# A stored order of all steps replaced by another, in a fused attention and two-layer feed-forward kernel

## The chip, the cores and the metric

The kernel runs on one core of a Trainium2 chip. The metric is the time of one execution on the device in microseconds (us). The profile is one such execution, recorded by the hardware profiler.

## What is computed

Three stages follow each other. Four batches of eight heads attend over 576 positions in a window (the first four heads: the last 32 positions; the other four: every fourth of the last 128). The result, 2304 tokens of 512 numbers, goes through a first feed-forward block with a softmax gate and a layer norm, and then through a second block with a GELU.

```
scores = scale * np.matmul(q, k.transpose(0, 1, 3, 2))          # 4 x 8 x 576 x 576
scores = np.where(masks[None, :, :, :], scores, -1000000000.0)
attn = softmax(scores);  x = np.matmul(attn, v)                 # 2304 x 512

h = x @ w_in                                                    # 512 -> 1024
solu = h * softmax(h)
ln = (solu - mu) / np.sqrt(var + 1e-06) * g_ln
x = ln @ w_out                                                  # 1024 -> 512

h = x @ w_in2                                                   # 512 -> 2048
g = h * (1.0 / (1.0 + np.exp(-1.702 * h)))
out = g @ w_out2                                                # 2048 -> 512
```

The weights and inputs arrive as 64-bit numbers where the table of inputs has them so; the kernel makes 32-bit floats of them itself.

## The kernel before

**Units of work.** The attention is cut into 20 units (four batches, five units each), numbered n = 0 to 19. A unit has scores `s` (L268, L280, with a mask added by two matmuls at L264 in the first two batches), a maximum, exponentials and sums on VectorE and ScalarE, a normalization `t` (L343, mostly GpSimd), a transpose `ptp` on TensorE (L351), a copy `pt`, and the product with the values `xt` (L381, L384). Its results are copied into `xr`. In the first feed-forward block 18 tiles of 128 tokens each have two halves of `h` (L522, 12 matmuls a half), a normalization that ends on GpSimd (L565), two transposes `lt` (L577), and then groups `y` (L599, 24 matmuls each). The second block (`hx`, `hz` at L721, `ox`, `oz` at L799) fills the second half of the time.

**Precision by parts.** Each 32-bit operand is split into a high and a low part, and three products are added. So the first weights come in eight pieces `w1r0` to `w1r7` of 1 MB (two loads of 512 KB each, L422). The pieces 0 to 3 hold `w_in`. Each is turned into 32-bit floats by L429 and L437 (ScalarE, or L433 on VectorE) and L441 (VectorE), then split into `wi_h` (L478) and `wi_l` (L491). The first half of the first tile, `h0`, needs the pieces 0 and 1, the units 0 to 3, and `xh0`, `xl0` (L505, L511); its second half needs the pieces 2 and 3.

**What sets the order.** Every step (a load, a matmul group, an elementwise operation) is added to a plan. The list `ORDER` holds the numbers of all 2440 steps in the order in which they are written into the program, and the dictionary `PICKS` chooses the engine where a step can run on more than one (0 is the first named). Neither is worked out when the kernel is built: both are stored. Each engine then runs its instructions in that order, and waits where an operand or a buffer isn't there.

```
pick = PICKS.get(len(self.works), 0) if ORDER else pick
one = [list(can)[pick]] if pick >= 0 else list(can)
...
for k, n in enumerate(ORDER):
    w = self.works[n]
```

**Loads.** All loads and stores are issued by SyncE (SP), one after the other. The tile `qk` has two buffers in turn, so a third `qk` load waits until the scores that read the first are done. The tile `v` has three. Two of the eight score loads of the first batches and two value loads go into parts of the tiles `y1_0` to `y1_2`, which are free until later, and need no such buffer.

**Fillers.** `stir` (L250) puts up to four bf16 matmuls of 512 columns, whose result is overwritten, ahead of a step before which the plan sees TensorE idle.

```
for _ in range(min(4, int(STIR * plan.gap / 4))):
    nc.tensor.matmul(bank.rearrange("p (o n) -> p o n", o=4), ident_b, x, start=True, stop=True)
```

Of the kernel before, what the change touches and what calls it, by code (L numbers as in the profile page):

```python
# [61 lines left out]
class Plan:  # L62
# [5 lines left out]
    def add(self, rank, eng, cost, fn, after=(), take=(), give=(), lag=None, also=(), port=False, pick=-1):  # L68
        lag = {"PE": 0.2, "POOL": 0.1}.get(eng, 0.06) if lag is None else lag
        can = {eng: (cost, fn, port and eng != "ACT" or eng == "POOL")}  # L70
        can.update({e: (c, f, port or e == "POOL") for e, c, f in also})
        pick = PICKS.get(len(self.works), 0) if ORDER else pick
        one = [list(can)[pick]] if pick >= 0 else list(can)
# [5 lines left out]
    def in_order(self):  # L79

        free, slots, given, taken = {}, dict(self.slots), {}, {}
        for k, n in enumerate(ORDER):
            w = self.works[n]
# [21 lines left out]
    def order(self):  # L105
        if ORDER:
            return self.in_order()
# [1158 lines left out]
def plan_sequence():  # L1266
# [29 lines left out]
    for b in range(1, B):  # L1296
        todo, k = items[b - 1], 0
        for u in range(UB):
# [42 lines left out]
QUADS = [0, 1, 2, 3, 4, 5, 6, 7]  # L1341
R2 = 100000
ULO_ANY = True
ORDER = [1, 8, 56, 57, 58, 5, 67, 68, 59, 60, 61, 0, 69, 70, 71, 46, 47, 10, 18, 87, 88, 89, 72, 73, 9, 266, 267, 268,
# [125 lines left out]
PICKS = {63: 1, 73: 1, 75: 1, 91: 1, 106: 1, 107: 1, 127: 1, 128: 1, 138: 1, 146: 1, 159: 1, 160: 1, 179: 1, 192: 1,  # L1470
# [121 lines left out]
```

## Time and profile before

| | us |
|---|---|
| median of 3 runs | 659.62 |
| lowest and highest of them | 656.92 and 660.81 |
| the profiled execution, its own time | 659.48 |
| its span, first to last instruction | 657.7 |
| TensorE matmul busy | 634.6 |
| VectorE busy | 450.9 |
| ScalarE busy | 352.4 |
| GpSimd busy | 293.2 |

The profiled execution's own time is 1.8 us above its span, and 0.14 us below the median. A busy TensorE is read with care: its matmuls are pipelined and their ends are modelled, so whether it loses time shows better in the distance from one matmul group to the next, in the chain of waits and in the timeline, than in its busy share.

### The profile page before, as it was taken

To read this page: it belongs to the slowest core of one execution; us is meant where nothing else is said; L and a number is where in the kernel's file an instruction comes from. 1 tells how busy PE (TensorE), PEld (TensorE's weight loads), DVE (VectorE), ACT (ScalarE), POOL (GpSimd) and SP (SyncE) were. 2 spreads that over 40 slices of the span, in tenths; PEclk is the share of its full clock that TensorE was granted. 3 is DMA by queue.
4 is the path that set the end of the run, shared out by engine and by line. 5 is a ranking of instruction groups with operands and counts; after the bars stand their busy time and mean duration, and the time that the engine had idled before them with its cause. 6 is when DMAs were issued, how large, how long until landed. Compare 5 with 4: busy or idle time off the path is not lost.

```text
span 657.7 us, 14874 instructions
## 1 busy us (share of the span) xinstructions
PE 634.6 (96%) x5877; PEld 594.8 (90%) x5877; DVE 450.9 (69%) x779; ACT 352.4 (54%) x765; POOL 293.2 (45%) x338
## 2 busy tenths in 40 slices
PE   7689999999999999999989989999999999999997
PEld 4467888788998989999989989999999999999987
DVE  3978896686856766887868869734467943447573
ACT  3667867675635565545546755324455531435552
POOL 1246665647547366555544124410426450224363
PEclk9889999999999999999999999999999999999999
DMA  8986468544538366967899999658799877679773
GB/s 303 406 300 217 162 211 294 174 146 161 164 120 258 136 205 222 339 220 220 287 330 350 360 309 344 211 172 301 247 292 295 290 244 225 227 251 344 251 236 124
DMA packets 65013, 163.56 MB, mean 249 GB/s; under 512 B 6960, under 2 KB 28592, under 8 KB 64944
## 3 DMA queue, kind: packets, MB, share of 16 engines
q1 hardware_dynamic: 64944, 162.62, 72.8%
q8 instruction: 46, 0.75, 0.5%
q14 instruction: 23, 0.19, 0.1%
HBM read 126.42 MB, written 36.18 MB: 247 GB/s over the span
## 4 chain that ended last, share of the span: by engine, by line
PE 89%; DMA 5%; DVE 3%; issue 1%; ACT 1%; SPq 0%; POOL 0%; ACTq 0%; POOLq 0%; DVEq 0%
PE y L599 16%; PE h L522 16%; PE oz L799 14%; PE hz L721 14%; PE hx L721 11%; PE ox L799 10%; PE lt L577 2%; DMA ws<-wdq 2%; PE xt L381 2%; PE s L268 1%; PE xt L384 1%; PE ptp L351 1%; DMA w1r<-in_w_in_dram 1%; DMA wo<-wdo 1%; DVE gs L767 1%
## 5 line engine op out<-in xcount | busy, mean ns | idle before, releaser
L764 ACT CAST gs<-g 128x384 fp32r<-128x384 f32 x168 | 85.1, 514 | 71.9 <-PE oz L799 28.1
L767 POOL TENSOR_TENSOR gs<-g,gs 128x384 fp32r<-128x384 f32 x51 | 56.6, 1116 | 114.8 <-ACT gs L764 108.8
L721 PE MATMUL hz<-yc,ws 128*128 128x384 f32 x492 | 97.8, 334 | 0.0
L767 DVE TENSOR_TENSOR gs<-g,gs 128x384 fp32r<-128x384 f32 x117 | 75.6, 664 | 30.5 <-ACT gs L764 29.8
L721 PEld LDWEIGHTS hz<-yc,ws 128*128 128x128 f32 x492 | 86.4, 188 | 0.2 <-issue 0.2
L599 PE MATMUL y<-lnh,wo_h 128*128 128x256 f32 x288 | 82.8, 288 | 0.4 <-issue 0.4
L599 PE MATMUL y<-lnl,wo_h 128*128 128x256 f32 x288 | 81.4, 283 | 0.0
L599 PE MATMUL y<-lnh,wo_l 128*128 128x256 f32 x288 | 81.4, 283 | 0.0
L721 PE MATMUL hx<-yc,ws 128*128 128x384 f32 x369 | 75.0, 335 | 1.8 <-DMA ws<-wdq 1.8
L750 ACT ACTIVATE g<-g 128x384 f32<-128x384 f32 x72 | 36.6, 523 | 59.9 <-DVE g L740 41.3
L760 POOL TENSOR_TENSOR g<-g,g 128x384 f32<-128x384 f32 x34 | 38.1, 1126 | 66.0 <-ACT g L750 42.1
L721 PEld LDWEIGHTS hx<-yc,ws 128*128 128x128 f32 x369 | 64.7, 188 | 2.6 <-ACT hl_('q', 7, 1)_0_4957 L655 1.2
L522 PE MATMUL h<-wi_h,xh 128*128 128x512 f32 x144 | 59.6, 414 | 0.9 <-DVE xh L505 0.9
L799 PE MATMUL ox<-gs,wo 128*128 128x384 f32 x288 | 55.4, 337 | 1.9 <-DMA wo<-wdo 1.9
L522 PE MATMUL h<-wi_l,xh 128*128 128x512 f32 x144 | 57.0, 396 | 0.0
L522 PE MATMUL h<-wi_h,xl 128*128 128x512 f32 x144 | 56.8, 395 | 0.0
L599 PEld LDWEIGHTS y<-lnl,wo_h 128*128 128x128 f32 x288 | 55.1, 191 | 0.7 <-issue 0.5
L599 PEld LDWEIGHTS y<-lnh,wo_h 128*128 128x128 f32 x288 | 55.1, 191 | 0.4
L799 PE MATMUL oz<-gs,wo 128*128 128x384 f32 x288 | 55.2, 336 | 0.0
L599 PEld LDWEIGHTS y<-lnh,wo_l 128*128 128x128 f32 x288 | 55.1, 191 | 0.0
L799 PE MATMUL oz<-gs,w 128*128 128x384 f32 x288 | 53.6, 337 | 0.5 <-DVE ou L811 0.5
L799 PEld LDWEIGHTS ox<-gs,wo 128*128 128x128 f32 x288 | 50.3, 188 | 2.5 <-DMA wo<-wdo 1.8
(398 smaller groups left out, 1319.9 us busy)
## 6 DMA issues: line engine op xcount, KB each, us to landing
wo<-wdo SPq DMA_DIRECT2D x48, 512.0 KB, 6.2
ws<-wdq SPq DMA_DIRECT2D x41, 512.0 KB, 6.0
w<-wdo SPq DMA_DIRECT2D x72, 256.0 KB, 5.8
ws<-wdq SPq DMA_DIRECT2D x41, 384.0 KB, 5.1
qk<-in_qk_dram SPq DMA_DIRECT2D x14, 528.0 KB, 5.2
v<-in_v_dram SPq DMA_DIRECT2D x14, 512.0 KB, 5.4
y<-in_w_in_dram SPq DMA_DIRECT2D x9, 512.0 KB, 4.9
wdq<-y SPq DMA_DIRECT2D x9, 512.0 KB, 3.9
```

The lines of the kernel that those rows point to most:

```text
L268: nc.tensor.matmul(ps[QB * j:QB * j + QB, h, m * KW:m * KW + KW], q_[rows, c:c + QB], k_[rows, c:c + KW], start=not masked, stop=not maske ...
L351: nc.tensor.transpose(ps[:, j * P:j * P + P], t[:, 2 * j:2 * j + 2, :].rearrange("p m k -> p (m k)"), ident)
L381: nc.tensor.matmul(o, w, pt[rows, x:x + QB].rearrange("p (r t) -> p r t", r=4), start=True, stop=True, tile_position=(64 * par, 64 * h))
L522: nc.tensor.matmul(hps[i][:, half, :], x[:, kt, :], w[:, kt, fs], start=(kt == 0 and j == 0), stop=(kt == KT - 1 and j == 2))
L577: nc.tensor.transpose(ps[:, j, :], es[i][:, f * P:f * P + P], ident)
L599: nc.tensor.matmul(yps[g, dm][:, 0:n], w[:, f, ds_], x[:, f, 0:n], start=(f == 0 and j == 0), stop=(f == NF1 - 1 and j == 2))
L721: nc.tensor.matmul(ps[:, 0:TB2], quad_weights(p, q, m, kk, a), yc2[m][:, x, kk, :], start=(m < 4 and kk == 0 and i == 0), stop=(kk == 1 an ...
L750: nc.scalar.activation(g_tile(q, 0, 0) if (half, b) == (0, 0) else src, src, AF.Gelu_apprx_sigmoid)
L760: eng.tensor_tensor(o_block(jj, *o), o_block(jj, *x), o_block(jj, *y_), op)
L764: nc.scalar.copy(gsp[jj, m][:, 0], o_block(jj, half, b))
L767: eng.tensor_tensor(gsp[jj, m][:, 1], o_block(jj, half, b), f32(gsp[jj, m][:, 0]), ALU.subtract)
L799: nc.tensor.matmul(ps, w, gsp[jj, m][:, x], start=m < 4 and first and i == 0, stop=last and i == 2, skip_group_check=True)
```

## The change

Only `ORDER` and `PICKS` are replaced. No step is added or removed. Of the 2440 places of `ORDER`, those that differ lie in the first part, up to the `y` groups of the third pair of token tiles; from there to the end the two lists are the same.

```
-ORDER = [1, 8, 56, 57, 58, 5, 67, 68, 59, 60, 61, 0, 69, 70, 71, 46, 47, 10, 18, 87, 88, 89, 72, 73, 9, 266, 267, 268,
+ORDER = [8, 1, 56, 57, 10, 58, 59, 60, 61, 5, 97, 98, 99, 9, 266, 267, 67, 268, 269, 270, 68, 62, 0, 46, 63, 100, 101,
...
-PICKS = {63: 1, 73: 1, 75: 1, 91: 1, 106: 1, 107: 1, 127: 1, 128: 1, 138: 1, 146: 1, 159: 1, 160: 1, 179: 1, 192: 1,
+PICKS = {54: 1, 75: 1, 85: 1, 86: 1, 96: 1, 104: 1, 138: 1, 139: 1, 149: 1, 157: 1, 159: 1, 160: 1, 192: 1, 203: 1,
```

The list is said to have been searched anew with the known phase and measured time of TensorE's instruction blocks. Three places show what that moves.

**The first loads, on SP.** Names: `qk4` here is the scores' operand of unit 5, `mk` the masks, `qkl0` and `vl0` belong to unit 4. Before:

```order
L886 DMA mk_103<-in_masks_dram 128x768
L225 DMA qk1_125<-in_qk_dram 128x1056
L221 DMA y1_0_77<-in_qk_dram 128x512
L222 DMA y1_0_77<-in_qk_dram 128x544
L225 DMA qk0_129<-in_qk_dram 128x1056
L225 DMA qk4_210<-in_qk_dram 128x1056
L237 DMA qkl0_215<-in_qk_last_dram 128x640
L239 DMA vl0_217<-in_v_last_dram 128x512
L422 DMA w1r1_270<-in_w_in_dram 128x1024 x2
L231 DMA y1_1_78<-in_v_dram 128x1024
L422 DMA w1r3_322<-in_w_in_dram 128x1024 x2
```

Now:

```order
L225 DMA qk1_124<-in_qk_dram 128x1056
L886 DMA mk_103<-in_masks_dram 128x768
L225 DMA qk4_127<-in_qk_dram 128x1056
L221 DMA y1_0_77<-in_qk_dram 128x512
L222 DMA y1_0_77<-in_qk_dram 128x544
L422 DMA w1r1_170<-in_w_in_dram 128x1024 x2
L225 DMA qk0_253<-in_qk_dram 128x1056
L221 DMA y1_0_77<-in_qk_dram 128x512
L222 DMA y1_1_78<-in_qk_dram 128x544
L422 DMA w1r3_275<-in_w_in_dram 128x1024 x2
```

The third `qk` load, which waits for the first scores, stood sixth, ahead of all weights; it now stands behind the first piece of `w_in`. Of the rest, the loads `qk6` and `y1_1` (values) stood ahead of the last `w_in` piece `w1r0` and now stand behind it.

**TensorE at the first half of `h0`.** `ptp5` and `s8` are a transpose of unit 5 and the scores of unit 8. Before:

```order
L351 MATMUL ptp5_710<-ident_67,t5_428 128x128 x4
...
L264 MATMUL s8_717<-mk_103,ident_b_72 128x256
...
L268 MATMUL s8_717<-qk7_638 32x64 x32
...
L250 MATMUL h0_763<-ident_b_72 128x512
L522 MATMUL h0_763<-wi_h_94,xh0_753 128x512
L522 MATMUL h0_763<-wi_l_95,xh0_753 128x512
```

Now:

```order
L351 MATMUL ptp4_703<-ident_67,t4_450 128x128 x2
...
L250 MATMUL h0_722<-ident_b_72 128x512
...
L522 MATMUL h0_722<-wi_h_94,xh0_708 128x512
L522 MATMUL h0_722<-wi_l_95,xh0_708 128x512
...
L264 MATMUL s8_767<-mk_103,ident_b_72 128x256
...
L268 MATMUL s8_767<-qk7_710 32x64 x32
```

`s8` and `ptp5` moved from ahead of the first half of `h0` to behind it, and four fillers instead of one stand before it.

**TensorE around `ptp10`.** `s16` and `xt12` are scores and values of the last two batches, `h6` a tile of the first block. Before (a row of 64x4x8 stands for one of 32 in a unit):

```order
L381 MATMUL xt12_0_2124<-pt12_2110,v10_1333 64x4x8
...
L268 MATMUL s16_2165<-qk13_1841 32x64 x32
L351 MATMUL ptp10_2202<-ident_67,t10_2004 128x128 x4
L351 MATMUL ptp17_2212<-ident_67,t17_1240 128x128 x4
L522 MATMUL h6_2091<-wi_h_94,xh6_1947 128x512
```

Now:

```order
L351 MATMUL ptp17_2094<-ident_67,t17_1386 128x128 x4
L268 MATMUL s16_2102<-qk13_1975 32x64 x32
L381 MATMUL xt12_0_2146<-pt12_2029,v10_764 64x4x8
...
L522 MATMUL h6_2189<-wi_h_94,xh6_1874 128x512
L522 MATMUL h6_2189<-wi_l_95,xh6_1874 128x512
...
L351 MATMUL ptp10_2217<-ident_67,t10_1982 128x128 x4
```

Half a tile of `h6` (12 matmuls), which stood ahead of `xt12`, now stands between `xt12` and `ptp10`.

In numbers over the whole program, 28 fillers stand where 27 did. By `PICKS`, GpSimd has three of the four `wi_l` splits instead of two and one `wi_h` cast instead of none; VectorE has one `wi_l` and one `wi_h` fewer; the two `wo_h` operations that GpSimd had are VectorE's.

## Rows read from the trace of the kernel before

**Rows 1.** The page: busy times, the instructions' queue, a load's KB and us to landing

```profile
PE 634.6 (96%) x5877; PEld 594.8 (90%) x5877; DVE 450.9 (69%) x779; ACT 352.4 (54%) x765; POOL 293.2 (45%) x338
...
q8 instruction: 46, 0.75, 0.5%
...
v<-in_v_dram SPq DMA_DIRECT2D x14, 512.0 KB, 5.4
```

**Rows 2.** By stretch: length, busy us (xinstructions) per engine, granted clock, DMA share, GB/s

```profile
0.00:41.10 41.10, 28.09 (x800) 17.86 (x800) 28.88 (x45) 23.48 (x63) 11.01 (x15) 0.96 0.96 349
41.10:150.00 108.90, 106.92 (x1869) 90.40 (x1871) 86.80 (x158) 79.62 (x198) 63.70 (x85) 0.98 0.60 205
...
300.00:400.00 100.00, 96.25 (x551) 95.06 (x550) 76.47 (x144) 57.63 (x117) 39.95 (x43) 1.00 0.94 319
```

**Rows 3.** The chain of waits that ended last: start us, us, what

```profile
41.12 4.61 PE h L522 x12
...
123.03 1.06 PE xt L381 x64
124.10 0.79 PE s L268 x53
124.89 0.48 PE ptp L351 x3
125.36 1.56 issue
...
147.15 2.75 PE h L522 x12
...
152.50 2.87 PE y L599 x24
...
324.77 8.54 DMA ws<-wdq
```

**Rows 4.** TensorE's timeline: stops that end with "issue"

```profile
12.78 0.52 PE L280 MATMUL s<-qkl 64*32 64x64 f32 x18 [0.94 <-issue]
...
27.22 1.26 PE L381 MATMUL xt<-pt,v 64*64 64x32 f32 x43 [2.61 <-issue]
...
126.92 0.75 PE L351 MATMUL ptp<-ident,t 128*128 128x128 f32 x5 [1.56 <-issue]
...
139.09 0.28 PE L599 MATMUL y<-lnh,wo_h 128*128 128x256 f32 x1 [0.41 <-issue]
```

**Rows 5.** By stretch, as rows 2, from one such stop to the next

```profile
18.83:27.20 8.37, 4.11 (x127) 2.69 (x127) 8.23 (x12) 4.71 (x6) 3.42 (x2) 1.00 1.03 409
27.20:33.40 6.20, 5.46 (x128) 3.52 (x128) 5.46 (x13) 4.17 (x15) 1.04 (x1) 0.72 1.03 406
```

**Rows 6.** By stretch, as rows 2, the first 10 us and the third

```profile
0.00:10.00 10.00, 7.40 (x177) 3.84 (x180) 3.04 (x6) 3.14 (x9) 1.01 (x8) 1.00 0.80 263
...
20.00:30.00 10.00, 5.74 (x142) 3.39 (x139) 9.69 (x16) 5.92 (x14) 2.25 (x2) 0.88 1.03 409
```

**Rows 7.** Timeline of all engines: start us, us, engine, line, what, [idle before]

```profile
2.58 3.87 SPq L225 DMA_DIRECT2D qk<-in_qk_dram  x2
...
33.54 1.17 ACT L429 ACTIVATE w1r<-w1r 128x1024 f32<-128x1024 f32 x1
...
34.44 2.41 POOL L491 TENSOR_TENSOR wi_l<-w1r,wi_h 128x1024 fp32r<-128x1024 f32 x1
...
34.82 2.58 DVE L433 TENSOR_SCALAR w1r<-w1r 128x1024 uint32<-128x1024 uint32 x1
...
38.68 0.38 PE L264 MATMUL s<-mk,ident_b 128*128 128x256 bf16 x2
...
39.78 0.39 PE L250 MATMUL h<-ident_b 128*128 128x512 bf16 x1
```

**Rows 8.** Groups by line and shape, first 60 us: xcount, busy us, mean ns, idle before

```profile
L433 DVE TENSOR_SCALAR w1r<-w1r 128x1024 uint32<-128x1024 uint32 x3 | 4.0, 1320 | 0.8 <-DMA w1r<-in_w_in_dram 0.8
L478 DVE CAST wi_h<-w1r 128x1024 fp32r<-128x1024 f32 x3 | 2.1, 694 | 0.1
```

94 rows, old and new, of tables (ORDER, PICKS) are left out of this document.

## The prediction

> **What bounds the kernel now.** I read the page first, then the stretches, then the chain of waits, then TensorE's timeline. On the page TensorE is busy for 634.6 of 657.7 us [rows 1]. The stretches show where the rest lies [rows 2]: 28.09 of the first 41.10 us, 106.92 of the next 108.90, and 96.25 of the 100 from 300 to 400. In between, TensorE is never idle. The chain of waits says the same: from 41.12 us on it is nearly all TensorE, with a DMA at 324.77 as the longest exception [rows 3]. So time can be had in two ways: the front, before the first half of `h0` runs, can be made shorter, or the small stops behind it can go. Both orders hold the same work, so what comes after changes place but not size.
>
> The stops are what the change is about. In the timeline TensorE stands for 0.94, 2.61, 1.56 and 0.41 us with the remark "issue": nothing that the profile shows held it [rows 4]. There are seven such places in all, five of them in the front. From one to the next the engine runs 127 or 128 matmuls and as many weight loads [rows 5], which with the waits of its own queue makes 256 instructions. The instruction queue brought 46 packets of 0.75 MB in all, 16 KB each, for twice 5877 instructions [rows 1]: one packet for 256. So TensorE stops where a block of 256 ends and the next hasn't come. In program order all seven fall at the same remainder by 256. Most of the 46 ends cost nothing. Those that do come soon after the block before, in work that uses up instructions fast: the one at 126.92 ended a block of some 2.3 us of work (a value product of 1.06, scores of 0.79, most of a transpose at 0.48) [rows 3]. In `h` 24 instructions last 2.75 us and in `y` 48 last 2.87 [rows 3]; a block with one of these in it lasts longer than its successor needs to arrive.
>
> The Trainium skill, "Runtime: NRT & Kernel Launch", section "Instruction fetch mechanics", says that crossing such a boundary is mostly hidden, since instructions are dispatched more slowly than blocks are fetched. By this rule the phase would be worth nothing; the trace agrees for most ends, and disagrees for seven of 46, with 0.41 to 2.61 us.
>
> **The change, part by part.** *The loads of the front.* SP stood 3.87 us at the `qk` loads, since the third needs a buffer of the first [rows 7]. In the first 10 us the DMA moved 263 GB/s, in the third ten 409 [rows 6]: it fell short by 146 x 10 / 409 = 3.6 us, of which I count 2.0 to the wait and the rest to the first load's own latency, as the first scores must wait for that in either order. The new order has 1 MB of weights to move meanwhile. Ahead of the last piece of `w_in` it also has `qk6` (528 KB) and a value tile (512 KB) less, 1.06 MB or 2.6 us at 409 GB/s. So the piece lands 2.6 to 6.2 us earlier, by my reckoning 4.6. The last value tile has the same loads ahead of it as before, and gains 2.0 alone.
>
> *The chain from there to `h0`.* ScalarE took up the last piece at 33.54 [rows 7], and TensorE began `h0` at 41.12 [rows 3]. VectorE was the engine without room: 8.23 of 8.37 us from 18.83 [rows 5], 9.69 of 10 from 20 [rows 6]. In the new order it has its first piece about 5 us earlier, where it had idle time (3.04 busy in the first ten), and one `wi_l` split and one cast (0.694, rows 8) fewer. Three block ends still lie on the way (in `xt0`, in `xt2`, and behind the first three instructions of `h0`); in the old order five did, the worst at 2.61 [rows 4]. Ends of the estimate: `h0` begins 6.2 us earlier, at 34.9, or not earlier at all, since VectorE was full. I take 3.6 earlier, 37.5: the 4.6 of the loads less 1.0, as the last end now lies in `h0` itself, where nothing else covers it.
>
> *The sum at `h0`.* The first half of `h0` took 4.61 us in the old trace, against 2.75 of the later halves [rows 3]; the granted clock of the front is 0.96 [rows 2], so part of it ran at 1.2 GHz instead of 2.4. I take 3.6, between the two. Then `s8` and `ptp5`, which stood ahead, are owed: 1.10 (from 38.68 to 39.78, rows 7) and 0.5 [rows 3]. The new order has done the same work at 37.5 + 3.6 + 1.6 = 42.7, the old one at 41.12 + 4.61 = 45.7. Gain 3.0; ends: 34.9 + 2.75 + 1.6 = 39.3, a gain of 6.4, and 41.1 + 4.6 + 1.6 = 47.3, a loss of 1.6. The one filler more stands in idle time; without that cover it costs a quarter of a microsecond.
>
> *The stops behind the front.* 1.56 at `ptp10` and 0.41 in `y1_0` [rows 4], on the chain with nothing beside them, 1.97 together. The old block before `ptp10` lasted 2.3 + 1.56 = 3.9 us. The new one holds most of `s16` (0.65), `xt12` (1.06) and eleven matmuls of `h6` (2.5): 4.2 us, so its successor should be there just in time. The next short one, some 4.6 us, holds one half of `h7` and two value products. With a full DMA a block lasted up to 8.37 us [rows 5], so new stops may cost 0 to 2; the DMA share here is 0.60 [rows 2], nearer to the cheap end. I take 0.6. Gain 1.4, between 0 and 2.0.
>
> *New waits.* About a thousand steps stand in another order between 41 and 150 us. VectorE is busy for 86.80 and ScalarE for 79.62 of 108.90 there [rows 2], so a step that comes 1 or 2 us late isn't always caught. The old order loses 108.90 - 106.92 = 1.98 us of TensorE there, hardly more than the two stops; a new one may lose 0 to 3 more. I take 0.8. Moved past others on SP: a store of split weights now stands ahead of the value load for `xt6`, so the load waits for GpSimd. TensorE reaches `xt6` some 9.5 us after the buffer is free (two halves of `h` and four short groups), which covers a load of 5.4 us to its landing [rows 1] if GpSimd isn't late by over 4.
>
> *Behind 150 us* the engines' orders agree but for a few places. The DMA at 324.77 is issued as TensorE gives a buffer free [rows 3], so it comes earlier by what TensorE has gained. Nothing takes the gain back unless the DMA itself is the bound there; its share is 0.94 from 300 to 400 [rows 2].
>
> Sum: -3.0 - 1.4 + 0.8 = -3.6 us. From the profiled execution, 659.48, that is 655.9; against the median of 659.62, 0.14 above it, 656.0.
>
> **The rivals.** *The front gives nothing* (0.20). VectorE was full from 18.83 to 30 [rows 5, 6], and earlier loads then only queue ahead of it. `h0` begins at 40.0 instead, the work is equal at 45.2, the gain there is 0.5: 659.5 - 0.5 - 1.4 + 0.8 = 658.4. Against it: VectorE's idle time in the first ten.
>
> *GpSimd becomes the bound, and it is slower* (0.10). It now makes three `wi_l` splits at 2.41 us [rows 7] and a cast that VectorE did in 0.694 [rows 8], between 0.7 and 2.4, say 2.0. And it holds VectorE up: in the old trace L433, started 0.38 us after a split on GpSimd, took 2.58 us and ended just after it [rows 7], where the mean of three is 1.320 [rows 8], so about 0.7 for the others, a loss of 1.9. Two such splits stood in the old front, four long operations in the new: 3.8 us more of VectorE, and 2.4 for the last split on GpSimd, which `h0` waits for. Then `h0` begins at 37.5 + 6.2 = 43.7, takes 4.61, and the work is equal at 49.9, a loss of 4.2: 659.5 + 4.2 - 1.4 + 0.8 = 663.1. It decides from a start of `h0` at about 40.1 on: later than that the kernel is slower. The Trainium skill, "SBUF — State Buffer", section "Who interferes with whom", has the same lock: of VectorE in certain modes and GpSimd the one that starts second waits for the whole instruction of the first. The trace agrees, with 2.58 us.
>
> *The front gives all that the loads do* (0.13): -6.4 - 2.0 + 0.4 = -8.0, 651.5. For it: the early half of VectorE's time is idle.
>
> *The blocks were never worth anything* (0.05): the stops are of another cause and come back elsewhere, so the 1.4 is lost and the front's gain stays: 659.5 - 3.0 + 0.8 = 657.3. Against it: the spacing of 256 [rows 5]. It is what the rule of the Trainium skill's page on the runtime, named above, would make of the time.
>
> **How the numbers follow.** The forecast has 0.52, with a range of its own from 653.5 to 658.5 (the front's gain between 1.5 and 4.5, the stops' between 0.5 and 2). About 0.5%, 3.3 us, is what a measurement of this kernel can tell from no change: faster means below 656.3. Of the forecast two thirds lie there, 0.34, and all of the third rival: 0.47. The rest of the forecast, the first and the last rival make 0.43 within 0.5%. Slower is the second rival, 0.10. The range from 652.0 to 661.0 leaves out most of that one and half of the third.
>
> **What would show it.** After: `h0` begins near 37.5 in the chain, the first ten microseconds move well over 263 GB/s, and the last piece of `w_in` is taken up before 30. No "issue" wait stands at `ptp10` or in a `y` group; where one stands, a block of less than 4.5 us went before it. From the point where `s8` and `ptp5` are done, TensorE's groups follow at the old distances. Wrong would be: `h0` after 40; L433 or an operation on small `sx` tiles at 2 us beside GpSimd's splits; TensorE waiting for VectorE, GpSimd or a value load between 45 and 110; or a DMA wait near 325 that has grown by what was gained.

## The result, and the profile after

In the comparison of the change itself the kernel before took 659.67 us (656.92 to 660.86, six executions) and the changed one 652.52 (651.11 to 654.36, six): a ratio of 0.990, 95% interval 0.9873 to 0.9927, or 7.1 us less. In the later comparisons below the kernel before came to 658.72, 658.66 and 659.19 (71 executions) and the changed one, run once more, to 652.99; so about 6 us is the better figure. The forecast was 656.0, a gain of 3.6. The direction held, and so did the outer range, 652.0 to 661.0, by half a microsecond. The forecast's own range, 653.5 to 658.5, did not: the gain was 1.7 to 2 times the forecast.

The page of after, its line of busy times and the queue of instructions (answering to [rows 1]; the span is 650.6, before 657.7):

```profile
PE 632.1 (97%) x5878; PEld 594.6 (91%) x5878; DVE 448.1 (69%) x778; ACT 351.8 (54%) x766; POOL 292.9 (45%) x338
...
q8 instruction: 46, 0.75, 0.5%
```

By stretch, as [rows 2]:

```profile
0.00:41.10 41.10, 28.67 (x742) 19.19 (x743) 28.54 (x47) 24.87 (x64) 17.77 (x19) 0.92 0.91 339
41.10:150.00 108.90, 108.31 (x2063) 92.54 (x2062) 88.83 (x159) 78.72 (x199) 58.57 (x83) 1.00 0.59 209
300.00:400.00 100.00, 98.69 (x566) 97.76 (x565) 80.39 (x148) 58.33 (x119) 42.63 (x44) 1.00 0.94 328
```

Busy time alone misleads in the front: 28.67 of 41.10 us is hardly more than before, since the clock there is lower (0.92) and a slow matmul is busy for longer. The other two stretches show less idle time: 0.59 us for 1.98 before, and 1.31 for 3.75. The first 10 us and the third, as [rows 6]:

```profile
0.00:10.00 10.00, 6.94 (x205) 3.73 (x205) 2.52 (x6) 2.12 (x3) 1.02 (x8) 1.00 0.82 297
20.00:30.00 10.00, 6.76 (x226) 4.61 (x214) 9.72 (x14) 8.24 (x22) 4.82 (x3) 1.00 1.03 409
```

The chain of waits of after, pieces that answer to [rows 3]:

```profile
38.72 2.92 PE h L522 x12
...
148.69 2.88 PE y L599 x24
...
330.84 6.33 DMA ws<-wdq
...
372.81 7.65 DMA wo<-wdo
```

The `y` group at 148.69 is the one that stood at 152.50 [rows 3]: TensorE is 3.81 us ahead there, and the same 3.8 at each group up to 325 us. The other 3.3 of the 7.1 between the two spans come behind that. A DMA's length in the chain runs from its issue to its landing, and TensorE works through most of it. So the waits themselves say more. The chain of before has a second load of `ws` behind the one at 324.77 [rows 3]:

```profile
335.82 7.03 DMA ws<-wdq
```

The 6.33 of after is this second one; the first ends no wait there. What TensorE waited for between 300 and 400 us, before and then after (us in total, times, longest):

```profile
PE ox L799 <- DMA wo<-wdo: 1.9, 2, 1.4
PE hx L721 <- DMA ws<-wdq: 1.8, 2, 0.9
```

```profile
PE ox L799 <- DMA wo<-wdo: 1.1, 1, 1.1
PE hx L721 <- DMA ws<-wdq: 0.3, 1, 0.3
```

At the same matmul the lead is 3.8 us up to 325 us, 5.0 behind the first wait for `ws`, 5.7 behind the second, 6.5 behind `wo`, and 7.1 at the end.

All that TensorE waited for between 45 and 150 us, in the view of waits (us in total, times, longest):

```profile
PE s L268 <- issue: 0.6, 1, 0.6
```

Before, the stops of 1.56 and 0.41 lay here [rows 4].

### The profile page after: what moved, and what is told of

Same layout as the page of the kernel before. It is cut to its first block, busy times and chain, and to the rows that moved or that the text cites. A ratio compares the mean times of both kernels' runs of the same rounds, so it can differ in the third digit from the quotient of the medians.

```text
span 650.6 us, 14875 instructions
## 1 busy us (share of the span) xinstructions
PE 632.1 (97%) x5878; PEld 594.6 (91%) x5878; DVE 448.1 (69%) x778; ACT 351.8 (54%) x766; POOL 292.9 (45%) x338
## 4 chain that ended last, share of the span: by engine, by line
PE 89%; DMA 3%; DVE 3%; ACT 1%; issue 1%; POOL 0%; SPq 0%; POOLq 0%; ACTq 0%
PE y L599 16%; PE h L522 16%; PE hz L721 15%; PE oz L799 14%; PE hx L721 11%; PE ox L799 9%; PE lt L577 3%; PE xt L381 2%; PE ptp L351 1%; PE xt L384 1%; PE s L268 1%; DMA wo<-wdo 1%; DMA ws<-wdq 1%; DVE gs L767 1%; DMA wdo<-hl_('o', 3, 1)_1_5307 1%
```

## The experiments

Each was timed in five rounds beside the kernel before; a ratio is to that. "Old" and "new" stand for before and after. In the two runs on the front `PICKS` goes with each step's order (in the first of them five steps from place 201 on also change places among themselves). These two keep the late weights in the old buffers, and the runs with a moved load or a changed pick keep the buffers of their own order, by a table that is explained below.

**The front alone.** `old` and `new` are the two lists:

```diff
-ORDER = new
+ORDER = new[:121] + [n for n in old if n not in new[:121]]
```

> The new order up to the second half of h0 (its first 121 places), then the steps that are left in the old order, with the old order's buffers for the late weight tiles. Theory A, the gains add up: in the trace of after the front is worth 2.7 us at the second half of h0, and that alone comes through, since the short block at ptp10 (some 1.9 us of work by the distances of the old trace) and the waits for weights between 325 and 390 us stay: 659.5 - 2.7 = 656.8, with an issue stop of 1.5 to 2 us near ptp10. Rival B, the front's lead also shortens the weight waits behind 300 us (4.8 us of TensorE lost there before, 2.1 after): 654. Rival C, the front gives nothing that lasts: 659.5.

666.52 us, ratio 1.0113 (1.0076 to 1.0150): none of the three. `h0` begins at 38.60, but then the chain of waits holds this:

```profile
39.36 8.68 DMA w1r<-in_w_out_dram
```

By the new order of the loads this piece (`w1r5`) comes late, and in the old order that follows VectorE takes it ahead of the sums of unit 8 and of unit 6. TensorE stands for 5.8 us ahead of `h1`, until VectorE's step L311 of unit 6 is done:

```profile
54.01 1.86 PE L250 MATMUL h<-ident_b 128*128 128x512 bf16 x4 [5.82 <-DVE t L311]
```

The front isn't a part that can be had by itself at this cut. A cut further ahead:

```diff
-ORDER = new
+ORDER = new[:90] + [n for n in old if n not in new[:90]]
```

> The first 90 places of the new order (the loads, and TensorE up to the values of unit 3), then the steps that are left in the old order, with the old buffers of the late weight tiles. No wait of TensorE comes with it by the plan's own clock, other than in front_only. Theory A, the front is worth 2.5 to 3 us alone and the stops stay: the block that ends behind ptp10 holds some 2.4 us of work, so an issue stop of about 1.5 us comes there; against the 658.7 of before in the last comparison 658.7 - 2.7 = 656.0. Rival B, the front's lead is lost again in waits between 45 and 110 us since the rest was ordered for another front: 658 or more.

657.48, ratio 0.9986 (0.9966 to 1.0005), 1.2 us less, which the interval doesn't tell from no change. `h0` begins 1.7 earlier than before, at 39.41. Two block ends ate part of it: TensorE's timeline of this kernel, at `s8` and at `s6`, and the stop that was expected at the end of the transposes:

```profile
38.38 0.27 PE L264 MATMUL s<-mk,ident_b 128*128 128x256 bf16 x1 [1.35 <-issue]
...
45.13 0.39 PE L268 MATMUL s<-qk 64*32 64x64 f32 x23 [1.42 <-issue]
...
125.39 0.49 PE L351 MATMUL ptp<-ident,t 128*128 128x128 f32 x3 [1.47 <-issue]
```

So the front does start `h0` earlier, and what is left of that depends on where the block ends fall in it.

**The blocks alone.** Short matmuls move every later end of 256 instructions, in the old order:

```diff
+        if i == 0 and half == 0:
+            for _ in range(16):
+                nc.tensor.matmul(hps[i][:, half, 0:32], ident_b, ident_b[:, 0:32], start=True, stop=True)
```

> The old order with 16 short matmuls of 32 columns ahead of the first half of h0, where TensorE stood 0.95 us. They move each later end of 256 instructions back by 32. Theory A, the blocks: the block that ended in ptp10 with 2.2 us of work ends behind s16 with 4.5, and the end before it lies in h6 and not in a value product; the stops of 1.56 and 0.41 us go: 658.7 - 1.9 = 656.8. Rival B, they are of another cause or come back at other ends: 658.7. What the short matmuls cost ahead of h0 is 0 to 0.5 us under either.

657.30, ratio 0.9978 (0.9956 to 1.0000), 1.4 us less, at the edge of what can be told from no change (the traced execution took 654.5). Both stops are gone, and a new one stands in `s10`, in the same view:

```profile
104.88 0.32 PE L268 MATMUL s<-qk 64*32 64x64 f32 x9 [1.04 <-issue]
```

And in the new order, the other way, with 40 of them ahead of `ptp3`:

```diff
+        if n == 3:
+            for _ in range(40):
+                nc.tensor.matmul(ps[:, 0:32], ident_b, ident_b[:, 0:32], start=True, stop=True)
```

> The new order with 40 short matmuls of 32 columns ahead of ptp3, where TensorE stood 3.1 us in the trace of after. They move every later end of 256 instructions back by 80 places: the block that ends in ptp11 then holds some 2.1 us of work and the one that ends in h6 some 2.3. Theory A, the phase of the blocks matters: where the old trace had a block of 2.3 us it stopped 1.56, so two stops of 1.5 to 2.0 us come behind the front, and the time is 652.5 + 3.5 = 656.0; without the stop of after near 75.6 us (0.8) it would be 655.2. Rival B, the stops are of another cause: no stop at these ends, 652.5. Beside it the short matmuls may keep the granted clock at 2.4 GHz from 32 us on, where after has 1.2 for 6.8 us, which takes 1 to 2 us off the front under either theory.

656.25, ratio 0.9964 (0.9945 to 0.9984). That is theory A's number, for another reason: no stop came at the two short blocks behind the front (1.8 and 2.4 us of work), and the loss lies in the front, where the short matmuls themselves ran out of instructions:

```profile
32.88 0.58 PE L352 MATMUL ptp<-ident_b 128*128 128x32 bf16 x17 [2.65 <-issue]
```

Not all of that loss is the edit's: a stop of 2.39 us stands in this trace ahead of the added matmuls, at an end that cost 0.98 in after.

So a short block isn't enough for a stop. I then took from ten traces the time at which each block's packet started, counted from the moment when TensorE was 30 instructions short of the end before (an estimate of how far its queue runs ahead: some packets start up to 3.3 us before TensorE is at that end). With no load in flight at that moment it started after 1.1 us (median of 74), with one after 1.7, two 3.1, three 3.6, four or more 4.8. The slope is firm and the figures are not: over all 46 ends of the same ten traces, with stores counted too, they are 0.9, 1.0, 1.9, 2.7 and 3.9. The stop at `ptp10` has two loads of 512 KB behind each other, issued 0.05 and 0.67 us after that moment, so a count at the moment itself misses them. Such a count shows only that the two go together. New theory: what stops TensorE is a short block that meets loads in flight. Its test moves one load on SP, and TensorE not at all; in the old order a raw weight of the second block, behind the next `qk` load:

```diff
 ORDER = [
-    ..., 682 (raw fetch), ..., 38 (qk12), ...
+    ..., 38 (qk12), 682 (raw fetch), ...
```

> The old order with one load moved on SP: a raw weight fetch (512 KB) that was issued 0.6 us behind a value load and landed 1.2 us behind it, around 120.8 us, now stands behind the next qk load. TensorE's queue came to the end before the block of ptp10 at about 120.1. Theory A, the loads in flight hold the block up: the block's fetch, which started 0.07 us after the value load landed, starts 1.0 to 1.3 earlier as that load now lands earlier; the stop at ptp10 falls from 1.56 (1.85 in the second trace of this order) to 0.2 to 0.6, and the time is 658.7 - 1.2 = 657.5. Rival B, a block that short stops TensorE whatever the loads do: 1.5 or more again, 658.7.

656.23, ratio 0.9955 (0.9937 to 0.9972), 3.0 us less. The transposes run through; TensorE's timeline here:

```profile
124.03 1.38 PE L351 MATMUL ptp<-ident,t 128*128 128x128 f32 x8
...
132.11 0.44 PE L268 MATMUL s<-qk 64*32 64x64 f32 x27 [1.29 <-issue]
```

The packet started 0.14 us after the end before, for 1.53 in the old trace, and the stop of 1.56 is 0.1. Rival B falls. The value load itself landed hardly sooner (4.1 us for 4.3), so that part of the expectation was wrong: it is the second load in flight that held the packet. In its place a stop of 1.29 stands at the next block's end, in `s15`; that the moved load causes it is likely, and no run shows it. TensorE is 1.3 us ahead at 151 us and 1.1 at the end of this trace, whose execution took 658.36. Where the rest of the 3.0 between the medians comes from stays open. The same in the new order:

```diff
 ORDER = [
-    ..., 752 (raw fetch), 35 (qk11), 28 (last unit), 32 (v9), 33 (qk10), ...
+    ..., 35 (qk11), 28 (last unit), 32 (v9), 33 (qk10), 752 (raw fetch), ...
```

> The new order with one load moved on SP: the fetch of a raw weight of the second block (512 KB), which stood ahead of the loads of qk11, the last unit, a value tile and qk10, now stands behind them. In ten traces so far the block of instructions was fetched about 1.1 us (median of 74 ends) after TensorE's queue came to the end before it where no load was in flight, and 3.6 to 4.8 us where three or more were; the stop in s13, 0.6 to 1.3 us in four traces of the new order, has five in flight, and its block is fetched just as the second of them has landed. Theory A, the loads in flight hold the block up: with one load less ahead the block comes 1.3 us earlier and the stop in s13 shrinks to 0.0 to 0.2; 652.8 - 0.7 = 652.1. Rival B, the delay has another cause: the stop stays at 0.5 to 1.3, 652.8.

651.90, ratio 0.9891 (0.9868 to 0.9915): the fastest median of all, 0.6 and 1.1 under the two of the changed kernel, but the intervals overlap, so the time doesn't tell it from them. The stop in `s13` is gone:

```profile
77.18 0.86 PE L268 MATMUL s<-qk 64*32 64x64 f32 x64
```

After has it in two pieces:

```profile
75.60 0.43 PE L268 MATMUL s<-qk 64*32 64x64 f32 x24
76.62 0.66 PE L268 MATMUL s<-qk 64*32 64x64 f32 x40 [0.59 <-issue]
```

The five traces with this block end and the load in its old place all have the stop, 0.5 to 1.3 us; the two with the load moved have none. Two things changed there, though. The loads that had stood behind the raw weight were issued 1.1 to 2.1 us earlier, and TensorE came to the end before 1.6 us later (72.53, for 70.94), as this trace has a stop that after lacks, at the end of a block in `h0`:

```profile
39.07 0.58 PE L522 MATMUL h<-wi_l,xh 128*128 128x512 f32 x1 [2.37 <-issue]
```

The moved load is issued some 30 us later and can't be its cause. So what this block end costs differs between executions, and in after nothing of it shows. Earlier loads and the later TensorE both give the packet of `s13` more room, and no run separates them.

**The buffers of the late weights.** Behind the differing places the two orders are the same, and yet the trace of after shows the load of one weight tile 6.9 us earlier where all else is 3.8 earlier. The buffer for such a tile is picked by the plan's own clock, which the earlier places shift: 28 of 194 tiles lie elsewhere. A table `BUFS` of the old choices, by the tile's name, takes that back:

```diff
+        k = BUFS[name]
         hl_until[k] = until
```

> The new order and picks, but each late weight tile (ws, hl, wo) in the buffer that the old program gave it, by a table of its 194 choices, of which 28 differ. Theory A, the buffers: in after the load of ws0_3_0_0 was issued 6.9 us earlier than before where everything around it was 3.8 earlier, since it lies in another buffer; with the old one the waits for ws near 330 and 340 and for wo near 380 are long again: 652.5 + 2.7 = 655.2. Rival B, the shorter waits come from TensorE being earlier, or from chance: 652.5.

654.67, ratio 0.9926 (0.9900 to 0.9953): about 2 us more than after by the medians, with an interval that overlaps both of the changed kernel's. SP's loads of after, and then of this kernel (0.9 us behind after on the whole):

```profile
306.40 0.32 SPq L668 DMA_DIRECT2D ws<-wdq  x1
```

```profile
310.41 0.32 SPq L669 DMA_DIRECT2D ws<-wdq  x1
```

The load is 3.1 us later by the buffer, and TensorE is idle for 2.66 of the 90 us from 310 to 400, where after has 1.31.

The other way, `BUFS` now holding the new program's choices:

```diff
-ORDER, PICKS = new
+ORDER, PICKS = old
```

> The old order and picks, with the new program's buffers for the late weight tiles. Theory A, the buffers: the waits for weights between 325 and 390 us shrink from 4.8 us of TensorE to some 2.1: 659.5 - 2.7 = 656.8. Rival B, they don't matter: 659.5.

657.22, ratio 0.9984 (0.9964 to 1.0004), 1.5 us less, and the same load is 3.1 earlier again. But the idle time from 310 to 400 us is 3.31 in its trace, hardly under the 3.75 of before. So both medians go the way of theory A, and neither is clear of noise. In the traces TensorE gains 2.7 us on before from 300 to 480 us in after, and 1.2 with the old buffers; in the old order it gains 0.7 with the new ones. Against theory A as the whole cause: the moved blocks, on the old buffers, gain 4.0 there in their trace.

**Chance.**

```diff
+# the same once more
```

> The changed kernel once more, nothing changed, for a second trace. Theory A, the shorter waits for weights between 320 and 400 us belong to the program: TensorE loses 2.1 us there again, give or take 0.5, and the time is 652.5. Rival B, they are chance: the loss lies anywhere from 2 to 5 us, as in the traces of five other kernels with the same steps there (2.75 to 4.8), and the times of single executions spread accordingly, over 3 to 4 us.

652.99, ratio 0.9910 (0.9891 to 0.9930). TensorE's idle time from 310 to 400 us is 1.17 here. Over all traces it is:

| order, buffers | idle of 90 us |
|---|---|
| old, old (before, and four kernels above) | 3.75, 3.03, 2.42, 0.58, 3.42 |
| old, new | 3.31 |
| new, old | 2.66 |
| new, new (after twice, and five kernels) | 1.31, 1.17, 1.94, 1.92, 1.43, 0.73, 0.83 |

The means of the first and the last row are 2.6 and 1.3. Four of the five traces of the first row lie above all of the last; the fifth (0.58, the moved blocks) lies below all of them. So the new order tends to wait less, but a single trace can't show it, and two executions of one program (1.31 and 1.17) are too few to say what chance alone does.

**GpSimd and VectorE.** One split back to VectorE:

```diff
-PICKS = {..., 275: 1, ...}
+PICKS = {...}
```

> The new order with one pick changed: the second split of w_in into wi_l (L491) on VectorE for GpSimd. In the trace of after that split ran on GpSimd from 25.81 to 28.22, and VectorE's smallest operation (L337, 128x4), started at 26.09, took 2.15 us for 0.17 to 0.2 of the others. Theory A, GpSimd held VectorE: L337 takes 0.2 again, VectorE has 2.0 us less to wait and 1.2 more to do, ptp3 and h0 come 0.7 earlier, 652.8 - 0.7 = 652.1. Rival B, L337 waits for something else: it stays long, VectorE has 1.2 more to do, and h0 is 1.2 later: 654.0.

652.05, ratio 0.9903 (0.9874 to 0.9932): like after. VectorE's timeline of after, and then of this kernel:

```profile
26.09 2.15 DVE L337 TENSOR_SCALAR sx<-sx 128x4 f32<-128x4 f32 x1
```

```profile
28.16 0.17 DVE L337 TENSOR_SCALAR sx<-sx 128x4 f32<-128x4 f32 x1
```

GpSimd did hold VectorE for 2.0 us, and without it the operation takes 0.17. But VectorE has the split of 1.2 instead, in this trace it also began that work 0.8 late, and `h0` starts at 38.55 for 38.16. What the hold cost is under 1 us.

**The clock.**

```diff
-            stir(ps[:, 0, :])
+            if n != 7:
+                stir(ps[:, 0, :])
...
+        if n == 3:
+            for _ in range(3):
+                nc.tensor.matmul(ps, ident, ident.rearrange("p (o n) -> p o n", o=1).broadcast_to([P, 4, P]),
+                                 start=True, stop=True)
```

> The new order with three 32-bit matmuls of 512 columns ahead of ptp3, where TensorE stood 3.1 us (28.8 to 31.9), and without the four fillers ahead of s7. Theory A, the clock: in the trace of after the granted clock is 0.5 from 32.1 to 38.9 us, after that wait; with work in it the clock stays 1.0, and the value products xt2 and xt3 take 1.06 us each as later ones do, for 1.73 and 1.84, and ptp3 0.5 for 0.88; h0 begins 1.8 earlier, at 36.3, and the time is 652.5 - 1.8 = 650.7. Rival B, the clock falls anyway, or h0 waits for the split on GpSimd that ends at 36.1 and for VectorE: 652.5. Rival C, the added matmuls themselves come in the way: 653.5.

653.79, ratio 0.9932 (0.9909 to 0.9955). The value products do run in 1.1 us, but the low clock (0.50) lies elsewhere now, ahead of them (stretches of this kernel):

```profile
25.00:31.80 6.80, 6.80 (x137) 4.76 (x138) 6.63 (x12) 5.63 (x16) 4.77 (x3) 0.50 1.00 385
31.80:38.90 7.10, 6.50 (x147) 4.38 (x146) 4.46 (x8) 4.79 (x15) 2.51 (x2) 1.00 0.80 269
```

That the three matmuls moved it isn't shown: it lies at 25.1 to 31.9 us also in the trace of the new order with one load moved, which doesn't have them.

`h0` begins at 37.58, 0.6 earlier and not 1.8, and a longer stop in `s13` (1.11) and the waits behind 300 us took more back. With the load moved as well:

```diff
+ both edits: the three matmuls ahead of ptp3, and 752 behind 33 in ORDER
```

> The new order with both: three 32-bit matmuls in the idle stretch ahead of ptp3 (as in the run on the warm front, where the second half of h0 began 0.85 us earlier and a longer stop in s13 took 0.6 of it back) and the raw weight fetch moved behind four loads. Theory A, both gains come through: 652.8 - 0.85 - 0.7 = 651.2. Rival B, what is gained ahead of 300 us is taken back by the waits for weights behind it, as in the warm front (0.26 us earlier at 225 us, 1.26 later at the end): 652.8 to 653.8.

654.63 (650.11 to 658.08), ratio 0.9927 (0.9903 to 0.9950). Neither rival: in this trace the lead is lost in front of `h0` and not behind 300 us. TensorE comes to the end in front of `h0` before its instructions do, as its timeline shows, while `w_out` is loading. It is the end that cost 2.37 in the run with the load alone, where TensorE also came to `h0` early (36.21, for 38.16 in after):

```profile
39.45 0.58 PE L250 MATMUL h<-ident_b 128*128 128x512 bf16 x1 [3.94 <-issue]
```

## Why the prediction was right, and where it was not

*The loads.* Right. The first 10 us move 297 GB/s for 263. The last piece of `w_in` has landed at 26.21, for 30.57 in the trace of before: 4.4 earlier, where I counted 4.6. ScalarE takes it up at 27.64, with L437, and by L429 at 28.69, for 33.54 [rows 7]; the timeline of after:

```profile
27.64 1.22 ACT L437 ACTIVATE w1r<-w1r 128x1024 uint32<-128x1024 uint8 x1
28.69 1.22 ACT L429 ACTIVATE w1r<-w1r 128x1024 f32<-128x1024 f32 x1
```

*The chain to `h0`, and its sum.* Right within 0.7. `h0` begins at 38.16 (forecast 37.5) and its first half lasts 3.41 to the next group (3.6), with one matmul at the low clock:

```profile
32.76 1.93 PE L381 MATMUL xt<-pt,y 64*64 64x32 f32 x64
34.48 1.91 PE L384 MATMUL xt<-pt,y 64*64 64x32 f32 x64
...
38.16 0.94 PE L522 MATMUL h<-wi_h,xh 128*128 128x512 f32 x1
```

The work is level at 38.16 + 3.41 + 1.6 = 43.2, for 45.7 before: a gain of 2.5, forecast 3.0. What I had not seen is that the clock's low stretch would lie ahead of `h0` this time, on two value products at 1.9 us each. The 1.0 that I counted for the block end inside `h0` did not come in this trace; at this end other traces lost 2.37 and 3.94, so that it cost nothing here was luck.

*The stops.* Right in the sum, with too simple a rule. 1.97 us went and one stop of 0.59 came, forecast 0.6; in four other traces with that end it was 0.5 to 1.3, so the match to the hundredth is luck. But I took a block's own length as what decides; the moved blocks showed blocks of 1.8 and 2.4 us without a stop, and one of 5.1 in `s13` with one. The moved loads show that loads in flight matter as well. No stop came at `ptp10`, as forecast, but not "just in time": the block's packet started at 119.18, with no load in flight, and the block was needed 3.9 us later, where at the old stop TensorE went on 2.4 us after the packet's start (124.55 to 126.92).

*New waits.* The 0.8 us did not come: between 45 and 150 us TensorE waits for nothing else. The load that stands behind a store, ahead of `xt6`, cost nothing. So at the `y` group of 148.69 us the gain is 3.81 where the three terms made 3.6. That they agree so well is luck in part: the front gave 0.5 less than forecast and the new waits cost 0.8 less.

*Behind 150 us.* This is the step that failed. I put it at nothing, since the orders agree, and as a risk only that the DMA wait near 325 might grow. That wait went, the next one for `ws` and those for `wo` shrank, and the two spans differ by another 3.3 us behind 325; by the medians of all executions it is about 2.2. That the lists agree there doesn't make the programs agree: the buffers of 28 weight tiles changed with the plan's clock, and one weight load came 3.1 us earlier by that. Undoing it cost about 2 us by the medians, not clear of noise. So the cause of the 2.2 stays open: the traces of the old order and buffers, kernels with different fronts, differ by up to 3.2 us in these waits, and no run separates the buffers, the lead of TensorE and chance.

*The rivals.* "The front gives all that the loads do" gave 651.5, nearer to the result than the forecast, but by a front gain of 6.4, and that is not what happened (2.5). "GpSimd becomes the bound" has its mechanism in the trace, at L337 and not at L433, with 2.0 us; VectorE and the rest of the front covered most of it. The Trainium skill, "SBUF — State Buffer", "Who interferes with whom", says that of VectorE in certain modes and GpSimd the second waits for the whole instruction of the first; the trace agrees, with 2.15 us beside a split of 2.41 that ended 0.02 us earlier, though no run shows the mode. "The blocks were never worth anything" is refuted, as to the cause of the stops, by the moved load, which took the stop of 1.56 away with TensorE's order as it was; that stops come back at other ends is true of several runs. The Trainium skill, "Runtime: NRT & Kernel Launch", "Instruction fetch mechanics", calls the crossing mostly hidden; the traces agree at most ends, above all where no load is in flight (about 1 us to the packet's start), and disagree where several are, with stops of up to 3.94 us in one.

*Parts and whole.* The front alone gave 1.2 us, the blocks alone 1.4, the buffers alone 1.5, each with an uncertainty of about as much; together 4.1 of 6. That they don't simply add up is what one would expect, as where the block ends meet the loads changes with each of them; with these uncertainties it isn't shown.

## What to carry to other kernels

Where TensorE runs many short matmuls, look at the stops that end with "issue": one can come where the end of 256 instructions meets loads in flight, and a load that isn't urgent, moved behind the next ones, can take it away without touching TensorE's order, or bring another at the next end. An order cut out of a searched one and joined to another can cost more than either, so change such a list in single steps. And where buffers are picked by a planner's clock, compare the buffers, not only the order, before a stretch is called unchanged.

## What the runs showed of the hardware

TensorE's instruction packets start later beside data loads: the median from TensorE's coming near the end to the start of the packet rose from about 1 us with no load in flight to between 3.9 and 4.8 with four or more, and moving one load of 512 KB took a stop from 1.56 to 0.1 us. The low clock (0.50, 1.2 GHz) came at another place in two executions of the same program: after has it from 32.1 to 38.9 us, the second trace of it also in the stretch ahead:

```profile
25.20:32.00 6.80, 6.01 (x139) 3.87 (x138) 6.44 (x11) 5.30 (x16) 4.86 (x3) 0.50 1.00 382
32.10:38.70 6.60, 6.60 (x139) 5.21 (x139) 3.64 (x7) 4.33 (x14) 2.41 (x1) 0.50 0.69 242
```

`h0` began at 38.16 and 38.27 all the same: ahead of 32 us TensorE had time to spare.
